# Doubles to single precision in two VectorE passes instead of three, inside an mLSTM and mixture-of-experts kernel

## The chip, the cores and the metric

One core of one Trainium2 chip. The metric is the device time of one execution in microseconds (us); lower is better. The core's engines are TensorE (PE in the profile; PEld is its weight load), VectorE (DVE), ScalarE (ACT), GpSimd (POOL) and SyncE (SP, which here only issues DMAs).

## The reference, cut to what matters

Three stages follow one another: an mLSTM attention with 4 x 8 heads over 768 positions and 40 columns a head, a dense two-layer network with 2048 hidden columns, and a mixture of 8 experts with one expert for each token.

```python
# attention, for every position t, in float32
m_new = np.maximum(f_gate[:, :, t] + m, i_gate[:, :, t])
C = f_stab[..., None, None] * C + i_stab[..., None, None] * np.einsum('bhd,bhe->bhde', vt, kt)
y[:, :, t] = o * np.einsum('bhde,bhe->bhd', C, qt) / denom
# dense layer: x is 3072 x 320
h = x @ w_in                                # w_in  320 x 2048
x = (h * (1.0 / (1.0 + np.exp(-h)))) @ w_out   # w_out 2048 x 320
# experts: one of 8 for each token, F = 1024
out[mask] = gate_w[mask, None] * (np.maximum(x[mask] @ w1[e], 0.0) @ w2[e])
```

The scale factor in `w_in` and `w_out` is a double, so both arrays come as doubles (64 bits an element), and the kernel first has to bring them to single precision. All other inputs are single precision.

## The kernel before, in words

The attention is computed in 6 chunks of 128 positions for 4 batches, which makes 24 tiles of 128 tokens (`unit(t)`). Each tile goes through the first dense layer (`l1`, `l1_two`), the second (`l2`, `l2_two`), the routing to an expert (`route`), and, sorted by expert in DRAM, through the experts (`slot`, `slot_two`). Values are split into a high and a low half-precision part (f16), and products are made of three terms of these parts.

Conversion of the doubles (`narrow`, L894) comes in 20 pieces of 128 x 512 elements. Ten are of `w_in` (`conv_in`, `conv_rest`), with two PSUM banks `cv_b` in turn and five staging tiles `t_b`. Ten are of `w_out` (`conv_out`), with the one PSUM bank `cvo_b` and three staging tiles `to_b`. A piece is loaded as pairs of 32-bit words into a staging tile T. Then VectorE makes a single-precision number in the PSUM bank by three passes on integers: L904 shifts the high word left by 3 and masks it, L907 adds the sign and the first exponent bit of the high word, and L910 adds the last three mantissa bits, which are the top bits of the low word. Behind that, the high f16 part is copied out (by ScalarE at L948, or by `scaled`, L75 on ScalarE and L77 on VectorE), TensorE subtracts it in the bank (`rest`, L923, and L970), and the remainder is copied out as the low part (`scaled` again). The first layer's products need the pieces of `w_in`; the second layer's need those of `w_out`.

The first 4 tiles (`unit(0)` to `unit(3)`) run beside the conversions. Their gates come from two scans for each part of the sequence (`gates`, L545 and L555, on VectorE), transposes (L594) and splits on GpSimd.

The order of the work is not the order of the program text. Each operation is entered with `op(engines, ns, ...)`: the engines that may do it, an estimated duration on each, what it reads and writes, a rank, and whether it uses the port that VectorE and GpSimd share in this model (`port`). `Plan.order` runs a list scheduler over the whole program eight times (`forward`, then new ranks from `backward`), keeps the shortest plan, and each engine executes its operations in that order. Where two engines are named, the plan also chooses the engine. The ranks of the first round come from the table `RK` (L28) and the position of the tile. Loads are issued on SP's queue in plan order, and each waits there until its buffer is free.

Of the kernel before, what the change touches and what calls it, by code (L numbers as in the profile page):

```python
# [10 lines left out]
F16 = mybir.dt.float16  # L11
BF16 = mybir.dt.bfloat16
I32 = mybir.dt.int32
AF = mybir.ActivationFunctionType
ALU = mybir.AluOpType
AX = mybir.AxisListType
# [9 lines left out]
SWG = 32.0  # L26
EX = 4
RK = dict(  # L28
    tiles=19.85, win=357.54, dwin=156.47, wout=226.1, dwout=-31.98, u0=-746.18, u1=-176.02, u2=-2598.68, u3=-1489.29,
    lead1=91.49, lead=1619.18, l1c=-760.87, l2c=-473.82, l2=-73.95, gates=-1631.02, load=-74.57, state=-183.26, route=-452.72,  # L30
)


# [5 lines left out]
def act(n):  # L39
    return 186 + 0.833 * n  # L40
# [6 lines left out]
def dve(n):  # L47
    return (n + 151) / 0.96


def pool1(n):
    return 85 + 1.3 * n
# [6 lines left out]
DP = ("DVE", "POOL")  # L59


def dp(n):
    return dve(n), pool2(n)
# [9 lines left out]
def scaled(nc, m, out, in_, scale):  # L73
    if m is nc.scalar:
        m.activation(out=out, in_=in_, func=AF.Copy, scale=scale)  # L75
    else:
# [211 lines left out]
def mlstm_moe_kernel(ctx, tc, q, k, v, ig, fg, og, w_in, w_out, w_gate, w1, w2, out):  # L288
    nc = tc.nc
# [18 lines left out]
    def op(*args, **kw):  # L308
        plan[0].op(*args, **kw)
# [27 lines left out]
    def pos(t):  # L337
        return T0 + TT * t
# [63 lines left out]
    for e in range(E):  # L402
        a = A[home[e]]
# [20 lines left out]
    fs, is_, ms, la, cl, rmask = [G0.cut([128, S], F32) for _ in range(6)]  # L424
    t_b = [A[0].cut([128, 1024], I32) for _ in range(5)]
    to_b = [A[1].cut([128, 1024], I32) for _ in range(3)]
    dg = A[1].cut([BH, NC, BH], F32)
# [10 lines left out]
    pe, ve, ac, po, sp = nc.tensor, nc.vector, nc.scalar, nc.gpsimd, nc.sync  # L438
# [68 lines left out]
    for e in sorted({e for e, _ in EARLY}):  # L507
        m = sum(1 for x in EARLY if x[0] == e)
# [12 lines left out]
       W=[("f", 0)], rank=-30, lag=2200, move=250)  # L521
    op("SP", 700, lambda: sp.dma_start(out=is_.ap[:, 0:CH], in_=bcast0(i2v[:, 0:CH], 128 // BH)),
       W=[("i", 0)], rank=-29, lag=2200, move=250)
    op("SP", 700, lambda: sp.dma_start(out=fs.ap[0:BH, CH:], in_=f2v[:, CH:]),
       W=[("f", 1)], rank=0, lag=2200, move=300)
    op("SP", 700, lambda: sp.dma_start(out=is_.ap[0:BH, CH:], in_=i2v[:, CH:]),
       W=[("i", 1)], rank=0, lag=2200, move=300)
# [115 lines left out]
    def unit(t):  # L643
# [3 lines left out]
        p = RK[f"u{t}"] if t < B else pos(t) - RK["lead1" if t < 2 * B else "lead"]  # L647
# [16 lines left out]
        if c > 0:  # L664
            op("SP", 450, lambda: [
                sp.dma_start(
                    out=lam[g].ap, in_=bcast0(lam_d[b * H + 4 * g:b * H + 4 * g + 4, c * CH:(c + 1) * CH], 128)
                ) for g in range(2)
            ], R=["lam_d"], W=[*lam], rank=ld + 3, lag=2500, move=1650)
            for g in range(2):  # L670
                op("POOL", pool1(512), lambda g=g: po.affine_select(  # L671
                    out=lam[g].ap, in_=lam[g].ap, pattern=[[0, 4], [1, CH]], compare_op=ALU.is_ge, fill=-1e30,
# [43 lines left out]
        for g in range(2):  # L716
            if c == 0:
                ps, kk = bank("at", 128, 4, CH)

                def first(g=g, ps=ps):  # L720
# [8 lines left out]
                   R=[kk], W=[lam[g]], rank=p + 2 + g)  # L729
            else:  # L730
                for j in range(4):
                    op("ACT", actp(128), lambda g=g, j=j: exps(4 * g + j, lam[g].ap[:, j, :]),
                       R=[("bias", 1)], W=[lam[g]], rank=p + 2 + g)

        if c > 0:
            op("ACT", act(H * D1), lambda: ac.activation(
                out=V2.ap[:, 0], in_=vr.ap, func=AF.Copy, scale=SQ
            ), R=[vr], W=[V2], rank=p + 4)
            op("DVE", dve(H * D1), lambda: ve.scalar_tensor_tensor(
                out=V2.ap[:, 1], in0=vr.ap, scalar=SQ, in1=V2.ap[:, 0], op0=ALU.mult, op1=ALU.subtract  # L740
            ), R=[vr], W=[V2], rank=p + 4, port=True)
        if c < NC - 1:
            op(DP, dp(H * D1), lambda m: m.tensor_tensor(
                out=vw.ap, in0=vr.ap, in1=wend_t[:, c, cols].unsqueeze(2).to_broadcast([128, H, D1]), op=ALU.mult
            ), R=[vr, ("wend", g_)], W=[vw], rank=p + 4, port=True)
        if 0 < c < NC - 1:
            op("ACT", act(H * D1), lambda: ac.copy(out=vv.ap[:, 0], in_=vw.ap), R=[vw], W=[vv], rank=p + 6)
            op(DP, dp(H * D1), lambda m: m.tensor_tensor(
                out=vv.ap[:, 1], in0=vw.ap, in1=vv.ap[:, 0], op=ALU.subtract
            ), R=[vw], W=[vv], rank=p + 6, port=True)  # L750
        op("ACT", act(320), lambda: ac.activation(out=orr.ap, in_=orr.ap, func=AF.Tanh, scale=0.5),
           W=[orr], rank=p + 8)
# [10 lines left out]
        for g in range(2):  # L763
            ps, kk = two[g]
            if c > 0:
# [6 lines left out]
                out=lam[g].ap, in0=ps, scalar=1.0 / SQ if c > 0 else SQ * SQ, in1=lam[g].ap,  # L772
                op0=ALU.mult, op1=ALU.mult
            ), R=[kk], W=[lam[g]], rank=p + 6 + g)
            if c == 0:
# [3 lines left out]
               R=[lam[g]], W=[P2], rank=p + 7 + g)  # L779
            op(DP, dp(512), lambda m, P2=P2, g=g: m.tensor_tensor(  # L780
                out=P2.ap[:, 1], in0=lam[g].ap, in1=P2.ap[:, 0], op=ALU.subtract
            ), R=[lam[g]], W=[P2], rank=p + 7 + g, port=True)
        if c > 0:
            it, ki = bank("at", 128, H, D1)

            def inter():
# [4 lines left out]
                out=hb.ap, in0=it, in1=E_t[:, c, cols].unsqueeze(2).to_broadcast([128, H, D1]), op=ALU.mult  # L791
# [15 lines left out]
        if c > 0:  # L807
            op("DVE", dve(H * D1), lambda: ve.tensor_tensor(out=pv, in0=pv, in1=hb.ap, op=ALU.add),
               R=[hb], W=[kv], rank=p + 10)

        def denom():
            nq = pv[:, :, D:D1]
            ve.tensor_scalar(
                out=dn.bitcast(I32), in0=nq.bitcast(I32), scalar1=0x7FFFFFFF, scalar2=None, op0=ALU.bitwise_and
            )
# [3 lines left out]
        y, ky = pv[:, :, 0:D], kv  # L819
        if c == 0:  # L820
            y, ky = hb.ap[:, :, 0:D], hb
            op(DP, (dve(160), pool1(320)), lambda m: m.tensor_scalar(
                out=orr.ap, in0=orr.ap, scalar1=1.0, scalar2=None, op0=ALU.add
            ), W=[orr], rank=p + 9, port=True)
            op(DP, dp(320), lambda m: m.tensor_tensor(
                out=orr.ap, in0=orr.ap, in1=den.to_broadcast([128, H, D]), op=ALU.mult
            ), R=[kd], W=[orr], rank=p + 11, port=True)
            op("DVE", dve(320), lambda: ve.tensor_tensor(out=y, in0=pv[:, :, 0:D], in1=orr.ap, op=ALU.mult),
               R=[kv, orr], W=[hb], rank=p + 11)
        else:  # L830
            op("DVE", dve(320), lambda: ve.scalar_tensor_tensor(
                out=y, in0=orr.ap, scalar=1.0, in1=y, op0=ALU.add, op1=ALU.mult
            ), R=[orr], W=[kv], rank=p + 11)
            op("DVE", dve(320), lambda: ve.tensor_tensor(
                out=y, in0=y, in1=den.to_broadcast([128, H, D]), op=ALU.mult
            ), R=[kd], W=[kv], rank=p + 11)
# [4 lines left out]
           W=[yy], rank=p + 12)  # L841
        op(DP if c == 0 else "DVE", dp(320) if c == 0 else dve(320), lambda m=ve: m.tensor_tensor(
            out=yl, in0=y, in1=yh, op=ALU.subtract
        ), R=[ky], W=[yy], rank=p + 12, port=c == 0)
        turned(yy, yy.ap.rearrange("p x c -> p (x c)"), xt, 6, p + 12, t < B - 1)
        if c < NC - 1:
# [15 lines left out]
            if c > 0:  # L862
                o = c * BH + b * H
                op(DP, dp(H * D1), lambda m: m.tensor_tensor(
                    out=C.ap, in0=C.ap, in1=dec[0:D, o:o + H].unsqueeze(2).to_broadcast([D, H, D1]), op=ALU.mult
                ), R=["dec"], W=[C], rank=rs - 4, port=True)
            op("PE", 24 * 30 if c else 920, state, R=[K, vv] if c else [kr, vw], W=[kk], rank=rs)
            if c > 0:
                op("DVE", dve(H * D1), lambda ps=ps: ve.scalar_tensor_tensor(
                    out=C.ap, in0=ps, scalar=1.0 / SQ, in1=C.ap, op0=ALU.mult, op1=ALU.add  # L870
                ), R=[kk], W=[C], rank=rs)
            else:
                op(AD, ad(H * D1), lambda m, ps=ps: scaled(nc, m, C.ap, ps, 1.0), R=[kk], W=[C], rank=rs)
            op("ACT", act(H * D1), lambda: ac.copy(out=Cs.ap[0:D], in_=C.ap),
               R=[C], W=[Cs], rank=rs + 4)
            op(DP, dp(H * D1), lambda m: m.tensor_tensor(
                out=cw.ap, in0=C.ap, in1=Cs.ap[0:D], op=ALU.subtract
# [9 lines left out]
    wpf = 2 if wide else 1  # L887
    win_v = w_in.bitcast(I32)
    wout_v = w_out.bitcast(I32)

# [3 lines left out]
    def narrow(T, X, mid, z, n, rank):  # L894

        if not wide:
            op("DVE", dve(n), lambda: ve.tensor_copy(out=z.ap.bitcast(I32), in_=T.ap[:, 0:n]), R=[T], W=[X, mid],
               rank=rank)
            return
        t4 = T.ap.rearrange("p (n w) -> p n w", w=2)  # L900
        lo, hi = t4[:, :, 0], t4[:, :, 1]
        a, m, o = X.ap.bitcast(I32), mid.ap.bitcast(I32), z.ap.bitcast(I32)
        sb = X.region != "PS"
        op("DVE", 150 + 0.78 * n if sb else dve(n), lambda: ve.tensor_scalar(  # L904
            out=a, in0=hi, scalar1=3, scalar2=0x3FFFFFFF, op0=ALU.logical_shift_left, op1=ALU.bitwise_and
        ), R=[T], W=[X], rank=rank, port=sb)
        op("DVE", dve(n), lambda: ve.scalar_tensor_tensor(  # L907
            out=m, in0=hi, scalar=-0x40000000, in1=a, op0=ALU.bitwise_and, op1=ALU.bitwise_or
        ), R=[T, X], W=[mid], rank=rank, port=sb)
        op("DVE", dve(n), lambda: ve.scalar_tensor_tensor(  # L910
            out=o, in0=lo, scalar=29, in1=m, op0=ALU.logical_shift_right, op1=ALU.bitwise_or
        ), R=[T], W=[X, mid], rank=rank, port=sb and mid is X)

    def opened():

# [526 lines left out]
    for t in range(2, B):  # L1442
# [4 lines left out]
       rank=12)  # L1447
# [33 lines left out]
    for t in range(1, NTT):  # L1481
# [24 lines left out]
        if t % B == 1 and t > 1:  # L1506
            next(ways, None)
            if t == NTT - B + 1:
# [3 lines left out]
                   R=["cum", "tri"], W=[kc], rank=pos(t) + 20)  # L1512
# [10 lines left out]
                for i, (e, n) in enumerate(EARLY):  # L1523
                    o = e * ER + 128 * (n + 1)
# [48 lines left out]
    def tabs():  # L1573
# [10 lines left out]
       rank=rk2)  # L1584

    def static_table():
# [9 lines left out]
       rank=rk2 + 1)  # L1596
# [126 lines left out]
```

## Time and profile before

| | |
|---|---|
| Median of 3 runs | 639.63 us (638.44 to 641.13) |
| Profiled execution | 638.35 us |
| Its span, from the first to the last instruction | 636.6 us |
| Mean granted TensorE clock | 0.988 |
| TensorE busy | 600.3 us, 94% of the span |
| VectorE busy | 488.2 us, 77% |
| ScalarE busy | 390.7 us, 61% |
| GpSimd busy | 309.8 us, 49% |

A row of a timeline gives start, duration, engine, line, operation, output and input, and in brackets the idle time of the engine ahead of it with what ended it. A row of waits gives who waited for whom, the total, how many times, and the longest. A row of a window table gives the stretch, its length, the busy time of each engine with the number of instructions, the granted TensorE clock as a share of full speed, the share of the 16 DMA engines, and GB/s.

### The profile page before, as it was taken

The page shows a single profiled execution, that of the slowest core. Times are in us where ns is not written, and L with a number is a line of the kernel's source. Part 1 is how long each engine was busy: PE and PEld are TensorE (multiplying, and loading weights), DVE is VectorE, ACT ScalarE, POOL GpSimd, SP SyncE. Part 2 cuts the span into 40 slices and gives each one's busy share as a digit, 9 for nine tenths or more (in the row PEclk, how much of TensorE's full clock was granted, in tenths as well). Part 3 has the DMA queues.
Part 4 walks back from the last instruction along what each step waited for, and adds up shares of the span by engine and source line. Part 5 has one row for each costly group of instructions (what it writes and reads, how often), then busy time and mean ns, then how long its engine had stood idle before and what let it go on. Part 6 is the DMA issues. An engine that isn't in the chain of part 4 may idle for free. (4 is left out here: it accounts for less than half of the span.)

```text
span 636.6 us, 17457 instructions
## 1 busy us (share of the span) xinstructions
PE 600.3 (94%) x6669; PEld 497.6 (78%) x6669; DVE 488.2 (77%) x986; ACT 390.7 (61%) x806; POOL 309.8 (49%) x462
## 2 busy tenths in 40 slices
PE   3889999999999989999999999999999899999992
PEld 2678888888888878878788887878788788888881
DVE  5997887889888788888798899757576675766660
ACT  2768897787778748888596755545432453644340
POOL 5537676557667568664764744511422214122311
PEclk9889999999999999999999999999999999999997
DMA  8999688999999969778876535582647889888610
GB/s 182 281 225 234 121 148 152 196 170 156 253 213 223 141 144 172 154 161 151 172 132 127 156 99 147 155 162 74 208 125 154 199 211 203 231 218 211 183 49 16
DMA packets 270006, 106.83 MB, mean 168 GB/s; under 512 B 207030, under 2 KB 265593, under 8 KB 269913
## 3 DMA queue, kind: packets, MB, share of 16 engines
q1 hardware_dynamic: 257176, 86.85, 67.1%
q10 hardware_dynamic: 9856, 10.10, 6.1%
q0 software_dynamic: 2880, 8.68, 3.8%
q8 instruction: 54, 0.88, 0.6%
q14 instruction: 40, 0.32, 0.2%
HBM read 68.76 MB, written 12.38 MB: 127 GB/s over the span
## 5 line engine op out<-in xcount | busy, mean ns | idle before, releaser
L1093 PE MATMUL PS<-A,A 128*128 128x256 f16 x1280 | 156.0, 272 | 0.6 <-DVE A L1097 0.6
L1093 PEld LDWEIGHTS <-A 128*128 128x128 f16 x1280 | 122.4, 98 | 17.6 <-issue 0.8
L1118 PE MATMUL PS<-A,A 128*128 128x320 f16 x320 | 95.7, 299 | 0.0
L1120 PE MATMUL PS<-A,A 128*128 128x320 f16 x320 | 95.6, 299 | 0.0
L1119 PE MATMUL PS<-A,A 128*128 128x320 f16 x320 | 95.6, 299 | 0.0
L1392 POOL DMA_INDIRECT out_dram<-W,sid x28 | 29.8, 1065 | 97.0 <-DVE W L1380 79.4
L1095 ACT ACTIVATE A<-PS 128x512 f32<-128x512 f32 x80 | 47.4, 594 | 36.5 <-PE PS L1093 31.2
L1097 DVE SCALAR_TENSOR_TENSOR A<-A,PS 128x512 f32<-128x512 f32 x80 | 54.1, 679 | 11.7 <-ACT A L1095 10.6
L1100 ACT CAST A<-A 128x512 f16<-128x512 f32 x80 | 49.1, 614 | 17.1 <-DVE A L1097 16.3
L712 ACT ACTIVATE A<-A,bias_t 128x128 f32<-128x128 f32 x160 | 56.0, 394 | 2.5 <-POOL A L671 2.4
L1416 PEld LDWEIGHTS <-A 128*128 128x128 f16 x512 | 49.7, 98 | 6.8
L1416 PE MATMUL PS<-W,A 128*128 128x256 f16 x448 | 52.7, 273 | 0.0
L1101 POOL TENSOR_TENSOR A<-A 128x512 f16<-128x512 f32 x28 | 35.1, 1254 | 31.6 <-ACT A L1100 31.6
L1354 PE MATMUL PS<-W,A 128*128 128x128 f16 x768 | 47.0, 219 | 2.6 <-DVE W L1358 1.8
L1354 PEld LDWEIGHTS <-A 128*128 128x128 f16 x768 | 44.8, 98 | 4.8 <-issue 3.1
L1418 ACT ACTIVATE W<-PS 128x512 f16<-128x512 f32 x32 | 19.1, 597 | 43.6 <-PE PS L1416 33.7
L1101 POOL TENSOR_TENSOR A<-A,A 128x512 f16<-128x512 f32 x24 | 28.5, 1188 | 29.7 <-ACT A L1100 28.2
L1356 ACT ACTIVATE W<-PS 128x512 f16<-128x512 f32 x24 | 14.2, 596 | 46.4 <-PE PS L1354 20.0
L771 DVE SCALAR_TENSOR_TENSOR A<-PS,A 128x512 f32<-128x512 f32 x48 | 32.2, 683 | 12.4 <-PE PS L769 11.3
L780 POOL TENSOR_TENSOR A<-A 128x512 f16<-128x512 f32 x25 | 31.5, 1259 | 19.2 <-ACT A L778 19.1
L1120 PEld LDWEIGHTS <-A 128*128 128x128 f16 x320 | 31.2, 98 | 12.2
L1430 PE MATMUL PS<-A,W 128*128 128x320 f16 x128 | 38.3, 299 | 0.5 <-DVE W L1380 0.5
(305 smaller groups left out, 1619.7 us busy)
## 6 DMA issues: line engine op xcount, KB each, us to landing
A<-lam_d SPq DMA_DIRECT2D x40, 256.0 KB
SG<-in_moe_w_dram SPq DMA_DIRECT2D x24, 320.0 KB
SG<-in_moe_w_dram SPq DMA_DIRECT2D x24, 256.0 KB
A<-in_moe_w_out_dram SPq DMA_DIRECT2D x10, 512.0 KB
A<-in_moe_w_in_dram SPq DMA_DIRECT2D x8, 512.0 KB
A<-in_k_dram SPq DMA_DIRECT2D x24, 160.0 KB
A<-in_q_dram SPq DMA_DIRECT2D x24, 160.0 KB
A<-in_v_dram SPq DMA_DIRECT2D x24, 160.0 KB
```

The lines of the kernel that those rows point to most:

```text
L712: ac.activation(out=lam[h // 4].ap[:, h % 4, :], in_=x, func=AF.Exp, bias=bias_t[:, c, b * H + h:b * H + h + 1])
L1093: pe.matmul(o, w[:, j, :], both[:, :, x, :], start=(n == 0), stop=(n == 7))
L1095: op("ACT", act(512), lambda: ac.activation(out=th.ap, in_=ps, func=AF.Tanh, scale=0.5 * HS), R=[kk], W=[th], rank=rk)
L1097: op("DVE", dve(512), lambda: ve.scalar_tensor_tensor(out=th.ap, in0=th.ap, scalar=1.0, in1=ps, op0=ALU.add, op1=ALU.mult), R=[kk], W=[th] ...
L1100: op("ACT", act(512), lambda: ac.copy(out=G.ap[:, 0], in_=th.ap), R=[th], W=[G], rank=rk + 2)
L1101: op(DP, dp(512), lambda m: m.tensor_tensor(out=G.ap[:, 1], in0=th.ap, in1=G.ap[:, 0], op=ALU.subtract), R=[th], W=[G], rank=rk + 2, port= ...
L1118: pe.matmul(ps, gh, w[:, 0, :], start=(f == 0), stop=False)
L1119: pe.matmul(ps, gh, w[:, 1, :], start=False, stop=False)
L1120: pe.matmul(ps, gl, w[:, 0, :], start=False, stop=(f == NF - 1))
L1354: pe.matmul(ps[:, jj, :], l, m, start=(n == 0), stop=(n == len(terms) - 1))
L1416: pe.matmul(o, a[:, k, :], both[:, :, x, :], start=(n == 0), stop=(n == 7))
L1430: pe.matmul(ps, hh[:, 0, 2 * f + b, :], x[:, 0, :], start=(g == 0 and f == 0), stop=False)
```

## The change

The second of the three passes is gone as a VectorE pass of its own. A new pass `three`, offered to GpSimd and ScalarE, reads the third 16-bit word of each double from above (the top half of the low word), scales it by 2^-13 with an offset that makes the rounding go down, and so writes its top three bits as an integer 0 to 7 into the low half of the high word, in place, in the staging tile. It comes behind the first VectorE pass, which still needs the old high word, and ahead of the last, which now takes the sign, the first exponent bit and these three bits from the high word with one mask. The masks of the first and last passes change to fit. The estimate for adding 1 to the output gate on GpSimd (L822) changes from 501 to 1012 ns, and all but one of the values in `RK` change, so the order of the whole program is computed anew.

```diff
@@ RK
-    tiles=19.85, win=357.54, dwin=156.47, wout=226.1, dwout=-31.98, u0=-746.18, u1=-176.02, u2=-2598.68, u3=-1489.29,
-    lead1=91.49, lead=1619.18, l1c=-760.87, l2c=-473.82, l2=-73.95, gates=-1631.02, load=-74.57, state=-183.26, route=-452.72,
+    tiles=19.85, win=453.55, dwin=151.6, wout=3.69, dwout=-20.45, u0=-751.86, u1=-141.04, u2=-3186.12, u3=-2421.48,
+    lead1=73.29, lead=1716.64, l1c=-997.71, l2c=-535.61, l2=-19.6, gates=-1783.78, load=-35.8, state=-251.22, route=-445.61,
@@ unit, chunk 0
-            op(DP, (dve(160), pool1(320)), lambda m: m.tensor_scalar(
+            op(DP, (dve(160), 1012), lambda m: m.tensor_scalar(
@@ narrow
-        lo, hi = t4[:, :, 0], t4[:, :, 1]
-        a, m, o = X.ap.bitcast(I32), mid.ap.bitcast(I32), z.ap.bitcast(I32)
+        hi = t4[:, :, 1]
+        a, o = X.ap.bitcast(I32), z.ap.bitcast(I32)
         sb = X.region != "PS"
         op("DVE", 150 + 0.78 * n if sb else dve(n), lambda: ve.tensor_scalar(
-            out=a, in0=hi, scalar1=3, scalar2=0x3FFFFFFF, op0=ALU.logical_shift_left, op1=ALU.bitwise_and
+            out=a, in0=hi, scalar1=3, scalar2=0x3FFFFFF8, op0=ALU.logical_shift_left, op1=ALU.bitwise_and
         ), R=[T], W=[X], rank=rank, port=sb)
+        t16 = T.ap.bitcast(U16).rearrange("p (n w) -> p n w", w=4)
+        low3, top = t16[:, :, 1], t16[:, :, 2]
+
+        def three(m):
+            if m is nc.scalar:
+                m.activation(out=top, in_=low3, func=AF.Copy, scale=2.0 ** -13, bias=-4095.5 * 2.0 ** -13)
+            else:
+                m.tensor_scalar(
+                    out=top, in0=low3, scalar1=4095.5, scalar2=2.0 ** -13, op0=ALU.subtract, op1=ALU.mult
+                )
+        op(("POOL", "ACT"), (85 + 3 * n, act(n)), three, W=[T], rank=rank, port=True)
         op("DVE", dve(n), lambda: ve.scalar_tensor_tensor(
-            out=m, in0=hi, scalar=-0x40000000, in1=a, op0=ALU.bitwise_and, op1=ALU.bitwise_or
-        ), R=[T, X], W=[mid], rank=rank, port=sb)
-        op("DVE", dve(n), lambda: ve.scalar_tensor_tensor(
-            out=o, in0=lo, scalar=29, in1=m, op0=ALU.logical_shift_right, op1=ALU.bitwise_or
-        ), R=[T], W=[X, mid], rank=rank, port=sb and mid is X)
+            out=o, in0=hi, scalar=-0x3FFFFFF9, in1=a, op0=ALU.bitwise_and, op1=ALU.bitwise_or
+        ), R=[T, X], W=[X, mid], rank=rank, port=sb)
```

## Rows read from the trace of the kernel before

**Rows 1.** Page, busy time of each engine, share of the span, instructions.
```profile
PE 600.3 (94%) x6669; PEld 497.6 (78%) x6669; DVE 488.2 (77%) x986; ACT 390.7 (61%) x806; POOL 309.8 (49%) x462
```

**Rows 2.** Windows by stage: length, PE, PEld, DVE, ACT, POOL, PEclk, DMA, GB/s.
```profile
0.00:20.00 20.00, 9.26 (x54) 5.88 (x54) 12.38 (x27) 7.24 (x15) 12.70 (x43) 1.00 0.91 197
20.00:60.00 40.00, 35.54 (x420) 30.27 (x421) 35.09 (x66) 28.73 (x61) 19.34 (x32) 0.91 1.02 245
60.00:100.00 40.00, 38.74 (x566) 33.51 (x564) 34.71 (x69) 34.96 (x83) 27.68 (x43) 1.00 0.73 147
100.00:620.00 520.00, 511.73 (x5601) 424.54 (x5600) 404.27 (x824) 319.74 (x651) 248.16 (x345) 1.00 0.78 167
620.00:636.60 16.60, 5.00 (x37) 3.38 (x35) 1.76 (x3) 0.00 (x0) 1.96 (x2) 0.74 0.05 16
```

**Rows 3.** First and last pass of `narrow`: ns minimum/median/maximum, first and last start.
```profile
L904 DVE TENSOR_SCALAR PS<-A x20: 673/686/695, 6.0 to 75.4; 128x512 int32<-128x512 int32 x20
...
L910 DVE SCALAR_TENSOR_TENSOR PS<-A,PS x20: 673/689/695, 9.7 to 79.5; 128x512 int32<-128x512 int32 x20
```

**Rows 4.** TensorE's waits: who for whom, total us, times, longest.
```profile
PE PS L594 <- DVE W L555: 3.0, 1, 3.0
...
PE PS L694 <- DVE PS L904: 1.5, 1, 1.5
PE PS L923 <- DVE A L77: 1.3, 1, 1.3
PE PS L1062 <- ACT A L75: 0.6, 1, 0.6
...
PE PS L1217 <- DVE cum L1212: 1.5, 1, 1.5
```

**Rows 5.** Windows of 4 us around TensorE's two gaps.
```profile
24.00:28.00 4.00, 1.98 (x19) 1.44 (x17) 4.00 (x8) 2.91 (x6) 2.31 (x5) 0.92 1.14 308
28.00:32.00 4.00, 4.00 (x35) 2.99 (x35) 3.93 (x8) 3.66 (x8) 0.74 (x1) 0.66 1.02 216
40.00:44.00 4.00, 2.25 (x18) 1.30 (x16) 3.96 (x9) 3.19 (x8) 1.16 (x3) 1.00 0.75 134
44.00:48.00 4.00, 4.00 (x33) 3.44 (x33) 4.00 (x8) 1.86 (x5) 1.98 (x3) 0.57 1.22 306
```

**Rows 6.** Timeline of VectorE, passes of conversions.
```profile
7.29 0.67 DVE L907 SCALAR_TENSOR_TENSOR PS<-A,PS 128x512 int32<-128x512 int32 x1
...
9.71 0.68 DVE L910 SCALAR_TENSOR_TENSOR PS<-A,PS 128x512 int32<-128x512 int32 x1
...
27.43 1.29 DVE L910 SCALAR_TENSOR_TENSOR PS<-A,PS 128x512 int32<-128x512 int32 x2
```

**Rows 7.** Windows of L904 alone (VectorE busy, count), and its fifth start.
```profile
0.00:20.00 20.00, 2.77 (x4) 1.00 0.91 197
20.00:60.00 40.00, 8.12 (x12) 0.91 1.02 245
...
20.38 0.68 DVE L904 TENSOR_SCALAR PS<-A 128x512 int32<-128x512 int32 x1
```

**Rows 8.** Groups by line: busy us, mean ns, idle before and releaser.
```profile
L1040 ACT CAST A<-A 128x512 f16<-128x512 f32 x6 | 3.7, 621 | 0.4 <-DVE A L1037 0.4
...
L822 POOL TENSOR_SCALAR A<-A 128x320 f32<-128x320 f32 x4 | 4.1, 1017 | 4.5 <-ACT A L751 4.5
...
L973 POOL COPY A<-SG 64x512 f16<-64x512 f16 x3 | 1.8, 609 | 0.1
```

**Rows 9.** Timelines of VectorE and GpSimd, one line with and without neighbour.
```profile
74.52 0.90 DVE L739 SCALAR_TENSOR_TENSOR A<-A 128x328 f16<-128x328 f32 x1
89.92 0.49 DVE L739 SCALAR_TENSOR_TENSOR A<-A 128x328 f16<-128x328 f32 x1
...
74.27 0.81 POOL L748 TENSOR_TENSOR A<-A,A 128x328 f16<-128x328 f32 x1 [0.24 <-ACT A L747]
...
90.20 1.24 POOL L780 TENSOR_TENSOR A<-A 128x512 f16<-128x512 f32 x1 [2.66 <-ACT A L778]
```

More of the change, by code (lines that the diff above doesn't have):

```diff
@@ L13 @@
 I32 = mybir.dt.int32
+U16 = mybir.dt.uint16
 AF = mybir.ActivationFunctionType
```

## The prediction

> **What bounds the kernel now.** I read the engine totals first, then the stages, then who TensorE waits for. TensorE is busy for 600.3 of the 636.6 us, far more than any other engine [rows 1]. The stage table tells where the other 36.3 us lie [rows 2]: 10.7 us in the first 20, 4.5 between 20 and 60, 1.3 between 60 and 100, 8.3 in the long stretch from 100 to 620, and 11.6 behind the last product. From 100 to 620 TensorE is busy for 511.7 of 520 us, so there the time is TensorE's work and little else; no VectorE pass that goes can shorten that work. What a faster VectorE can win lies before 100 us, and that is where all 20 conversions of the doubles are: their passes start between 6.0 and 79.5 us [rows 3], and VectorE is busy there for 35.1 of the 40 us from 20 to 60 [rows 2].
>
> TensorE's waits before 100 us give the places [rows 4]. It waits 3.0 us for the gate scan (L555), 1.5 us until a conversion's first pass lets a PSUM bank go (L904), 1.3 us for a half-precision copy of a converted weight (L77 on VectorE), and 0.6 us at the second layer's first products of a tile for a copy of the output weights (L75 on ScalarE). The second loss is the clock. In the stretch from 24 to 28 us TensorE is busy for only 2.0 of 4.0 us, and from 28 to 32 the granted clock is 0.66; from 40 to 44 it is busy for 2.3, and from 44 to 48 the clock is 0.57 [rows 5]. [...]
>
> **The change part by part.** *VectorE passes.* Each conversion had three passes of 128x512, 20 of each kind, 0.69 us at the median of the first and the last kind [rows 3]; two in a row take 1.29 us, so one more costs 0.60 [rows 6]. Twenty go: 12.0 us of VectorE time, of which 12 x 0.60 = 7.2 us between 20 and 60, where 12 conversions are opened [rows 7]. The mask of the first pass and the operands of the second change nothing in their form: 0 us.
>
> *The added pass.* Twenty passes of 512 16-bit elements, 8 bytes apart, in SBUF, on GpSimd or ScalarE, whichever the written order finds free. No row has this form. On ScalarE the nearest row is an SBUF-to-SBUF cast of 128x512 at 0.62 us [rows 8]; I take 0.6, bounded by 0.6 and, if the step halves the rate, 1.2. On GpSimd the nearest is the one-input arithmetic pass of L822, 1.02 us for 320 elements; by length 512/320 x 1.02 = 1.63 us. The bounds are the 512-element copy at 0.61 us and, since two operations are asked where L822 has one, twice 1.63 = 3.3 us. I take 1.6. ScalarE is busy for 28.7 and GpSimd for 19.3 of the 40 us from 20 to 60 [rows 2], so half of the passes on each (some 6 x 0.6 = 3.6 and 6 x 1.6 = 9.6 us there) finds room. That cover is gone where a pass stands in front of a copy for which TensorE waits.
>
> [...]
>
> *The chain of one conversion.* Two passes on one engine become VectorE, other engine, VectorE. Three passes took 0.60 + 0.60 + 0.69 = 1.9 us; now it is 0.69 + 0.6 + 0.69 = 2.0 us by ScalarE and 0.69 + 1.6 + 0.69 = 3.0 by GpSimd, before any queueing. So a conversion is longer by 0.1 to 1.1 us (2.8 at the upper bound), while its PSUM bank and its staging tile are held, and the loads behind it in SP's in-order queue wait as much longer.
>
> *The order.* The starting ranks in RK, the cost given for the +1 on the output gate, and the new operation enter the order that is computed for the whole program. The +1 passes are four of 1.02 us on GpSimd [rows 8]; on VectorE they would be under 0.7 us each (the price of a 512-element pass). For the moved ranks I set 0 us. The bounds are the idle time that an order can make or mend after 100 us: at best its 8.3 us would go [rows 2], and at worst as much comes in again; by the single wait, 1.5 us at L1217 [rows 4] is what one misplaced step costs, and I take both signs as equally likely.
>
> *The sum, against the profiled execution.* Gate scan: of the three passes of the first conversion, two stand between the scans (L907 at 7.29, L910 at 9.71 us [rows 6]); one goes, -0.6 us. The two waits on VectorE between 20 and 60: the passes removed before 24 us (five conversions opened [rows 7], 5 x 0.60 = 3.0 us) exceed the first wait of 1.5, and the next 4 us removed exceed the second of 1.3, so both go, -2.8. Of the 3.4 us lost at the lower clock I take half, -1.7, because other short waits remain there. From 60 to 100: the last 20 - 4 - 12 = 4 passes of 0.60 go [rows 7], but only 1.3 us of idle time is there to win; -0.5. What is late next: one conversion by GpSimd on TensorE's path, +1.2 (the 1.1 of the chain and 0.1 of hand-over). Together -4.4 us. The profiled execution took 638.35 us in all, 1.75 beyond its span, so it would take 633.95; the median of the runs is 639.63, 1.28 above the profiled one, so I forecast 639.63 - 4.4 = 635.2 us.
>
> **The rivals.** *Nothing passes through.* VectorE's passes were hidden, or the loads take their place: the DMA engines' share is 1.02 from 20 to 60 us [rows 2]. For it: the serial path of the first batches goes through all engines. Against it: the two waits name VectorE. Then only the 0.6 of the gate scan is left, about 639.0 us.
>
> *Everything goes.* Both gaps, all of the low clock behind them, and both passes ahead of the gate scan: 2.8 + 3.4 + 1.2 + 1.3 us = 8.7, so 630.9 us.
>
> *The port.* A VectorE pass with two SBUF inputs is stretched when GpSimd works: L739 takes 0.90 us beside GpSimd's L748 and 0.49 with GpSimd idle [rows 9], a difference of 0.41. If each of ten GpSimd passes met one such VectorE pass, 4.1 of the 12.0 us saved would be paid back and the gain shrinks to 4.4 x 7.9 / 12.0 = 2.9: 636.7 us. Against it: the conversion's own passes read or write PSUM and take 0.69 us everywhere, and two-input SBUF passes crowd only after 60 us. [...]
>
> *Slower: the output weights come late.* All ten output conversions share one PSUM bank, so their chains are serial, and TensorE already waits 0.6 us for one of them (L1062 [rows 4]), so there is no slack at that point. If the last three, after 60 us, go by GpSimd at 1.6 us behind its masks and subtractions, each is 1.1 us later, 3.3 us in all; TensorE has run out of first-layer products, idles that long and loses another 1.7 at the lower clock as behind the earlier gaps. With nothing won earlier but the gate scan that is +4.4: 644.0 us. It decides from the point where the added delay exceeds what the saved VectorE time brought forward; at GpSimd's upper bound of 3.3 us it would be twice the idle time.
>
> **How the numbers follow.** My forecast has 0.45, with a range of its own from 632.0 to 637.5; nothing passes through 0.20; everything goes 0.10; the port 0.10; the output weights 0.15. The 0.5% that a measurement of this kernel can tell is 3.2 us, so faster means under 636.4 and slower over 642.8. Faster: 0.40 of the forecast's 0.45, all of "everything", 0.05 of the port: 0.55. Slower: the output weights and a little for a bad order, 0.17. The rest, 0.28, is the same. The range runs from 630.5, just below "everything goes", to 642.5, which leaves out most of the slower rival.
>
> **What would show it.** Right: two passes of 0.69 us per conversion on VectorE, VectorE's busy time down by 13 us; TensorE's idle time before 100 us down from 16.5 to about 12; the stretches at a low granted clock between 24 and 48 us shorter; the time after 100 us unchanged to 2 us. Wrong: GpSimd's added pass over 2 us or TensorE's waits naming it; a wait at L1062 of several us; VectorE less busy before 60 us but TensorE idle as long as before; or idle time after 100 us that moved by more than all of these.

## The result and the profile after

The changed kernel takes 650.25 us at the median (648.75 to 650.56) against 639.04 for the kernel before beside it: a ratio of 1.0142 (95% interval 1.0108 to 1.0175), where 635.2 was forecast with a range up to 642.5. The profiled execution's span is 648.9 us, 12.3 more than before, and its mean granted clock 0.974.

The engines' totals of the kernel after, to be laid beside [rows 1]:

```profile
PE 605.7 (93%) x6668; PEld 500.4 (77%) x6669; DVE 491.1 (76%) x984; ACT 402.9 (62%) x811; POOL 324.9 (50%) x459
```

VectorE should have lost 13 us and has 2.9 more. Twenty passes are gone, but before 100 us its busy time falls by 5.3 us only, because the new order gave it other work (six passes of L1050 there instead of two, 4.5 us more): GpSimd is 15.1 us busier although its added passes alone take 22.6. Behind 100 us VectorE is 8.2 us busier, partly with the same passes: the 24 of L1221 take 10.2 us instead of 5.1. The stages answer to [rows 2], with the same columns:

```profile
0.00:20.00 20.00, 9.70 (x54) 6.00 (x54) 11.70 (x29) 10.00 (x16) 9.87 (x36) 1.00 0.87 205
20.00:60.00 40.00, 30.86 (x314) 25.36 (x316) 29.79 (x52) 29.10 (x51) 27.47 (x24) 0.74 1.05 239
60.00:100.00 40.00, 37.82 (x542) 33.18 (x542) 35.40 (x63) 35.19 (x73) 30.34 (x48) 1.00 0.75 132
100.00:620.00 520.00, 510.78 (x5598) 422.88 (x5596) 404.55 (x827) 323.54 (x666) 252.42 (x346) 1.00 0.80 167
```

TensorE's idle time grew from 36.3 to 43.2 us, by 6.9: before 100 us from 16.5 to 21.6, 4.7 of these 5.2 between 20 and 60, and by 1.7 behind 100 us. The other 5.4 of the 12.3 us are TensorE's busy time, 605.7 us instead of 600.3 for the same products. The granted clock between 20 and 60 fell from 0.91 to 0.74. By these shares alone that is 40 x 0.17 = 6.8 us, but they count the lower clock also where TensorE stood idle. That the clock makes up all of the 5.4 is not shown: a version below (no pass added, first set) is busy for 604.8 us with a clock of 0.91 in that stretch. VectorE, which was to be relieved, is the less busy one in that stretch, 29.8 us against 35.1: the time was not lost to a full VectorE, but to waits and the clock.

The two engines' versions of the added pass (all their instructions: minimum, median and maximum in ns, first and last start), the last pass as a group, and the waits behind it:

```profile
L913 ACT ACTIVATE A<-A x12: 1336/1358/1402, 5.6 to 89.3; 128x512 uint16<-128x512 uint16 x12
L915 POOL TENSOR_SCALAR A<-A x8: 2659/2695/3738, 17.5 to 80.9; 128x512 uint16<-128x512 uint16 x8
```

```profile
DVE PS L919 <- POOL A L915: 5.0, 5, 2.2
...
DVE PS L919 <- ACT A L913: 2.6, 2, 1.4
...
PE PS L932 <- ACT A L76: 8.3, 2, 6.3
PE PS L640 <- POOL A L841: 3.3, 1, 3.3
```

The added pass takes 1.36 us on ScalarE and 2.70 on GpSimd. The order reckons with 0.61 and 1.62. VectorE, which executes in its written order, waits 7.6 us for it (L919 is the last pass), and TensorE waits for copies that stand behind it on the two engines. Both places can be followed. First ScalarE, then TensorE, in timelines:

```profile
24.37 1.34 ACT L913 ACTIVATE A<-A 128x512 uint16<-128x512 uint16 x1
25.73 1.21 ACT L76 ACTIVATE A<-PS 64x512 f16<-64x512 f32 x2
```

```profile
26.99 1.07 PE L932 MATMUL PS<-A,less 128*128 128x512 f16 x2 [2.03 <-ACT A L76]
...
48.95 0.29 PE L640 MATMUL PS<-ident,A 128*128 128x128 f16 x1 [3.29 <-POOL A L841]
```

TensorE waits 2.03 us for a copy by L76 that comes right behind an added pass (the other 6.3 us of L932's wait lie at the first conversion, where the kernel without the added pass, below, has 6.1). The second wait, of 3.29 us, is for GpSimd's L841, a copy of 0.24 us. GpSimd's and VectorE's timelines ahead of it:

```profile
41.34 3.74 POOL L915 TENSOR_SCALAR A<-A 128x512 uint16<-128x512 uint16 x1
45.14 0.18 POOL L583 COPY A<-W 32x5 f32<-32x5 f32 x1
45.41 0.45 POOL L584 TENSOR_TENSOR A<-A,ident 32x160 f32<-32x160 f32 x1
45.94 2.66 POOL L915 TENSOR_SCALAR A<-A 128x512 uint16<-128x512 uint16 x1
48.65 0.24 POOL L841 COPY A<-A 128x64 f16<-128x64 f16 x1
```

```profile
40.96 1.64 DVE L556 TENSOR_TENSOR_SCAN W<-W 32x640 f32<-32x640 f32 x1
...
48.63 0.70 DVE L919 SCALAR_TENSOR_TENSOR PS<-A,PS 128x512 int32<-128x512 int32 x1 [2.23 <-POOL A L915]
```

Two added passes run with hardly a gap from 41.34 to 48.60, 7.3 us, which the order reckons as 2 x 1.62 and small work; L841 and VectorE's last pass, which waited for the second of them, both begin at 48.6. Behind these two gaps the clock is low, as behind those of [rows 5]; windows of the same form:

```profile
20.00:24.00 4.00, 3.83 (x22) 3.24 (x23) 3.22 (x9) 2.26 (x4) 1.62 (x3) 0.62 1.15 301
24.00:28.00 4.00, 1.97 (x18) 1.25 (x16) 2.62 (x5) 3.93 (x7) 1.21 (x2) 0.50 1.19 251
28.00:32.00 4.00, 3.03 (x21) 2.20 (x20) 3.05 (x5) 3.18 (x6) 3.21 (x3) 0.60 1.16 304
...
44.00:48.00 4.00, 1.54 (x15) 0.98 (x14) 1.46 (x3) 1.87 (x4) 3.77 (x4) 0.61 1.13 242
48.00:52.00 4.00, 2.32 (x13) 1.53 (x15) 3.26 (x7) 2.56 (x6) 3.80 (x7) 0.50 1.20 230
52.00:56.00 4.00, 4.00 (x37) 3.46 (x36) 1.92 (x4) 3.28 (x5) 2.42 (x3) 0.61 1.08 245
```

From 44 to 52 us TensorE is busy for 3.9 of 8 us, and until 56 the clock stays between 0.50 and 0.61. The first low stretch begins already in the window from 20, ahead of the gap at 24.

### The profile page after: what moved, and what is told of

Same layout as the page of the kernel before. It is cut to its first block, busy times and chain, and to the rows that moved or that the text cites. A ratio compares the mean times of both kernels' runs of the same rounds, so it can differ in the third digit from the quotient of the medians.

```text
span 648.9 us, 17478 instructions
## 1 busy us (share of the span) xinstructions
PE 605.7 (93%) x6668; PEld 500.4 (77%) x6669; DVE 491.1 (76%) x984; ACT 402.9 (62%) x811; POOL 324.9 (50%) x459
## 4 chain that ended last, share of the span: by engine, by line
PE 71%; DVE 12%; POOL 5%; issue 5%; DMA 3%; ACT 1%; SPq 1%; another core or an unknown queue 0%; ACTq 0%; POOLq 0%; DVEq 0%
PE PS L1102 17%; PE PS L1425 8%; PE PS L1127 5%; PE PS L1129 5%; PE PS L1128 5%; PE PS L1363 5%; PE PS L1439 2%; PE PS L1440 2%; PE PS L1441 2%; PE PS L1042 2%; POOL A L915 2%; PE PS L1376 2%; PE PS L1378 2%; PE PS L1377 2%; DVE A L1106 1%
## 5 line engine op out<-in xcount | busy, mean ns | idle before, releaser
L1109 ACT CAST A<-A 128x512 f16<-128x512 f32 x80 | 48.7, 614 | 16.5 <-DVE A L1106 15.8
L781 POOL TENSOR_TENSOR A<-A 128x512 f16<-128x512 f32 x34 | 41.6, 1226 | 19.7 <-ACT A L779 19.7
L1110 POOL TENSOR_TENSOR A<-A 128x512 f16<-128x512 f32 x26 | 31.6, 1216 | 26.5 <-ACT A L1109 23.5
```

Source lines behind the costliest of these rows:

```text
L1109: op("ACT", act(512), lambda: ac.copy(out=G.ap[:, 0], in_=th.ap), R=[th], W=[G], rank=rk + 2)
L1110: op(DP, dp(512), lambda m: m.tensor_tensor(out=G.ap[:, 1], in0=th.ap, in1=G.ap[:, 0], op=ALU.subtract), R=[th], W=[G], rank=rk + 2, port= ...
```

## The experiments

Theory: the added pass is longer than the order reckons with, stands in front of other work on two in-order queues, and TensorE idles and then runs at the lower clock, as in the windows above. Rivals: the new ranks made a bad order, or the split of a conversion over two engines costs by its hand-overs. Ratios are to the kernel before, run on the same chip in the same rounds.

**Order alone.** The three passes of before, with the new ranks and the new price of L822:

```diff
-    tiles=19.85, win=357.54, dwin=156.47, wout=226.1, ...
+    tiles=19.85, win=453.55, dwin=151.6, wout=3.69, ...
```

> The three VectorE passes of before, with the changed start ranks and the changed price of the +1 pass. Theory A (the added pass is longer than the order reckons with: 2.7 us on GpSimd and 1.36 us on ScalarE in the changed kernel's trace, against 1.62 and 0.61 in the order): there is no added pass here, so about the time of before, 637 to 642 us. Theory B (the new start ranks give a poor order whatever the passes cost): 647 to 652 us. Theory C (a conversion that hands over to another engine and back holds VectorE's in-order queue, however long the added pass is): 637 to 642 us.

636.36 us against 636.94, ratio 0.9994 (0.9975 to 1.0012). For three passes the new ranks are as good as the old ones; the ranks lose nothing by themselves, only together with the added pass.

**The pass cut to its price.** The changed kernel, its order untouched; the pass works on fewer elements:

```diff
-                m.activation(out=top, in_=low3, ...
+                m.activation(out=top[:, 0:186], in_=low3[:, 0:186], ...
-                    out=top, in0=low3, ...
+                    out=top[:, 0:302], in0=low3[:, 0:302], ...
```

> The changed kernel in its own order, but the added pass covers only the first 186 elements on ScalarE and the first 302 on GpSimd, so that it should last the 0.61 and 1.62 us that the order reckons with (by 2.3 and 5.1 ns per element); the last three mantissa bits of the other elements are left wrong. Theory A: the loss is gone, 633 to 640 us. Theory B: 647 to 652 us, the order is the same. Theory C: most of the loss stays, 645 to 650 us.

637.67 us against 636.94, ratio 1.0007 (0.9987 to 1.0028). The pass in this kernel:

```profile
L913 ACT ACTIVATE A<-A x12: 616/624/652, 5.6 to 85.2; 128x186 uint16<-128x186 uint16 x12
...
L915 POOL TENSOR_SCALAR A<-A x8: 1677/1694/2748, 16.7 to 76.1; 128x302 uint16<-128x302 uint16 x8
```

All hand-overs are still there, and the whole loss is gone: it came from the length of the pass. VectorE's waits for the pass fall from 7.6 to 2.4 us. But the forecast gain does not come either.

**One engine at a time.** The first cut alone on GpSimd (302 elements), then alone on ScalarE (186).

> The changed kernel in its own order, with only GpSimd's eight added passes cut to 302 elements (1.7 us instead of 2.7); ScalarE's twelve keep 512 (1.36 us). The last three mantissa bits of the elements left out stay wrong. Theory A1 (GpSimd's passes carry the loss: in the changed kernel's trace VectorE waits 5.0 us for them, and TensorE 3.3 us for a copy that stands behind one in GpSimd's queue): 637 to 642 us. Theory A2 (ScalarE's passes carry it): 646 to 650 us. If both add up: 642 to 646 us.

> The same with only ScalarE's twelve passes cut to 186 elements (0.62 us instead of 1.36); GpSimd's eight keep 512. Theory A1: 646 to 650 us. Theory A2: 637 to 642 us. If both add up: 642 to 646 us.

645.20 and 644.10 us against 640.21; ratios 1.0077 (1.0048 to 1.0106) and 1.0054 (1.0025 to 1.0084). From 1.0142 the cut on GpSimd takes 0.65%, that on ScalarE 0.88%; together 1.53%, which ends at 0.9989, where both cuts at once gave 1.0007. Within these intervals of 0.3% the two excesses add up, and neither engine's (12 x 0.74 us on ScalarE, 8 x 1.0 on GpSimd) is shown to weigh more.

**No added pass at all,** the order untouched (the operation is planned and issues nothing):

```diff
         def three(m):
+            return
```

> The changed kernel in its own order with no added pass at all: the last three mantissa bits of the converted weights are left wrong, and each conversion is two VectorE passes with nothing between. Theory A (only the length beyond what the order reckons with costs): 634 to 638 us, about the 637.7 us of the run with the pass as long as reckoned. Theory C (the hand-over to another engine and back costs by itself): clearly under that run, 628 to 634 us.

638.95 us against 640.21, ratio 0.9982 (0.9959 to 1.0005). So the forecast's best case in this order, two passes of VectorE and nothing added, is worth 0.2%, at most 0.4% and perhaps nothing. It is 0.25% under the run with the pass cut to its price, inside the intervals, so the hand-overs by themselves cost little, and the 628 to 634 us of theory C did not come. Its stretch from 20 to 60 us, and windows of 4 us, below them two windows of the kernel before:

```profile
20.00:60.00 40.00, 36.59 (x407) 31.15 (x408) 32.84 (x63) 27.57 (x55) 13.68 (x19) 0.83 1.00 232
...
16.00:20.00 4.00, 3.34 (x31) 2.32 (x28) 2.78 (x6) 2.15 (x4) 0.74 (x1) 1.00 1.07 356
20.00:24.00 4.00, 4.00 (x30) 3.52 (x31) 3.30 (x9) 1.46 (x3) 1.32 (x2) 0.56 1.15 296
24.00:28.00 4.00, 3.34 (x20) 2.24 (x19) 3.79 (x8) 3.17 (x7) 1.17 (x3) 0.50 1.09 244
```

```profile
16.00:20.00 4.00, 3.42 (x37) 2.54 (x35) 3.88 (x8) 3.19 (x6) 3.78 (x4) 1.00 1.12 254
20.00:24.00 4.00, 3.63 (x39) 3.02 (x40) 3.93 (x8) 2.62 (x7) 2.24 (x5) 1.00 1.08 340
```

Idle time between 20 and 60 us fell from 4.5 to 3.4 us, but the clock there is 0.83 instead of 0.91: by these shares 40 x 0.08 = 3.2 us more lost. Over the whole span TensorE idles 32.8 us instead of 36.3 and is busy for 603.0 instead of 600.3: of 3.5 us won in waits 2.7 are paid back as longer busy time. The clock falls in the window from 20 although TensorE was busy for 3.34 of the 4 us before it (3.42 in the kernel before, where it did not fall).

**The pass by itself.** A kernel of nothing but such passes, four of each form; it computes nothing of the reference:

```
ac.activation(out=u4(a0, 2), in_=u4(a0, 1), func=AF.Copy, ...)   # L44: as in the kernel
ac.activation(out=u1(a1),    in_=u4(a0, 1), ...)                 # L48: written densely
ac.activation(out=u4(a1, 2), in_=u1(a0), ...)                    # L50: read densely
ac.activation(out=i2(a1, 0), in_=u4(a0, 1), ...)                 # L54: 32-bit words written at the same step
```

> No part of the computation: nine forms of the pass on ScalarE and nine on GpSimd, four times each, 512 elements, nothing beside them. Theory P1 (the write of 2 bytes at a step of 8 is what costs): on ScalarE 1.36 us wherever the output is 16-bit at a step, 0.6 us for a dense or a 32-bit output; on GpSimd likewise less with a dense output. Theory P2 (the read at a step costs): 0.6 us with a dense input whatever the output. Theory P3 (16-bit integers cost, at any step): 1.36 us for all 16-bit forms, 0.6 for 32-bit floats. On GpSimd also: if the second operation costs, the one-operation form at the same steps is under 2 us.

Groups by line (busy us, mean ns, idle time before). L44 to L54 as above; GpSimd: L65 as in the kernel, L69 written densely, L71 read densely, L73 both dense, L75 one operation instead of two:

```profile
L65 POOL TENSOR_SCALAR P<-P 128x512 uint16<-128x512 uint16 x4 | 10.7, 2666 | 4.0 <-DVE P L22 3.7
...
L71 POOL TENSOR_SCALAR P<-P 128x512 uint16<-128x512 uint16 x4 | 10.5, 2628 | 0.3
L75 POOL TENSOR_SCALAR P<-P 128x512 uint16<-128x512 uint16 x4 | 8.9, 2215 | 0.3
L69 POOL TENSOR_SCALAR P<-P 128x512 uint16<-128x512 uint16 x4 | 7.8, 1946 | 0.3
...
L73 POOL TENSOR_SCALAR P<-P 128x512 uint16<-128x512 uint16 x4 | 7.7, 1923 | 0.3
...
L44 ACT ACTIVATE A<-A 128x512 uint16<-128x512 uint16 x4 | 5.5, 1377 | 0.0
L50 ACT ACTIVATE A<-A 128x512 uint16<-128x512 uint16 x4 | 5.3, 1335 | 0.1
...
L54 ACT ACTIVATE A<-A 128x512 int32<-128x512 uint16 x4 | 2.6, 661 | 0.1
...
L48 ACT ACTIVATE A<-A 128x512 uint16<-128x512 uint16 x4 | 2.6, 656 | 0.1
```

The write is what costs: 16-bit elements written 8 bytes apart take 0.7 us more than written side by side, on both engines (1377 against 656, 2666 against 1946 ns), and 32-bit words at the same step do not on ScalarE (661). The read at that step is nearly free (1946 against 1923). On GpSimd the second operation adds another 0.45 (2666 against 2215), though the one-operation form is not under 2 us as expected.

**Another write, in the kernel.** 32-bit words over the low word, all else as after:

```diff
-        low3, top = t16[:, :, 1], t16[:, :, 2]
+        low3, top = t16[:, :, 1], t4[:, :, 0]
```

> The changed kernel with its own order and prices; the added pass reads the same 16-bit words, but writes 32-bit integers, one over each whole low word, instead of 16-bit ones into half of the high word, so the last three mantissa bits stay those of the high word. The passes measured alone (m1_forms) give it 0.66 us on ScalarE and about 1.95 us on GpSimd, instead of 1.36 and 2.7. Theory (the time is lost to the 16-bit write at a step of 8 bytes): ScalarE's pass takes 0.65 to 0.70 us, GpSimd's 1.9 to 2.2, VectorE's waits for them fall from 7.6 us to under 2, and the time is 638 to 642 us beside 639 for the kernel before. Rival (it is the engine change as such, or the read of the half words, that costs): 646 to 651 us, with passes as long as before.

641.56 us against 641.04, ratio 1.0028 (0.9999 to 1.0057). All its added passes:

```profile
L913 ACT ACTIVATE A<-A x12: 657/676/702, 4.8 to 82.7; 128x512 int32<-128x512 uint16 x12
...
L915 POOL TENSOR_SCALAR A<-A x8: 1979/1999/3064, 15.7 to 72.8; 128x512 int32<-128x512 uint16 x8
```

Same engines, same order, same 512 elements and same reads: inside the kernel too the passes are as short as the form of the write makes them, and most of the loss is gone. But the edit takes away more than the form. The last pass does not read the low words, so it no longer waits for the added pass (VectorE's waits for it are gone, from 7.6 us), and the added pass no longer waits for the first: on ScalarE it begins at 4.78 us, ahead of VectorE's first pass at 4.86, where in the kernel after it begins at 5.63, behind it. GpSimd's and VectorE's timelines for the conversion whose last pass waited 2.23 us in the kernel after:

```profile
41.13 1.98 POOL L915 TENSOR_SCALAR A<-A 128x512 int32<-128x512 uint16 x1
41.16 0.68 DVE L919 SCALAR_TENSOR_TENSOR PS<-A,PS 128x512 int32<-128x512 int32 x1
```

So this run confirms the price of the write, but its time does not part the shorter pass from the hand-over that is gone. What ties the loss to the length is the run with the pass cut to its price, which keeps the hand-overs.

**True prices, and old ranks.** The order is told 2700 and 1360 ns with the ranks of after; and the ranks of before with the prices of after:

```diff
-        op(("POOL", "ACT"), (85 + 3 * n, act(n)), three, ...
+        op(("POOL", "ACT"), (2700, 1360), three, ...
```

> The changed kernel with the order computed from the measured prices of the added pass (2700 ns on GpSimd, 1360 ns on ScalarE). Theory A: the order now places the pass where there is room, so most of the loss is gone, 636 to 644 us; what remains is the real work, 20 times 0.75 to 1.1 us more than reckoned. Theory B and theory C: 646 to 652 us.

> The changed kernel with the start ranks of before; the added pass keeps its low prices in the order. Theory A: still late, 645 to 652 us. Theory B: the loss is gone, 636 to 641 us. Theory C: 645 to 652 us.

659.59 us, ratio 1.0361 (1.0313 to 1.0409), and 661.93, ratio 1.0418 (1.0366 to 1.0469). Both lie above every range that was expected. A true price alone made it worse, and so did the old ranks: the ranks were good for the program and the prices they stood with. In the first of these VectorE's waits for GpSimd's pass did fall to 1.9 us, but TensorE idles for 16.6 us from 100 to 620 instead of 9.2 in the kernel after, 7.7 of it far behind the conversions, at a single step of the experts (in the second, VectorE waits 9.4 us for GpSimd's pass instead of 5.0):

```profile
PE PS L1439 <- ACT W L1427: 7.7, 1, 7.7
```

**Ranks fitted anew.** To part the pass from the order, ranks were fitted by a search, twice each for the true prices, for two passes with nothing added (last three mantissa bits zero), and for the three passes of before (with the new price of L822).

> The changed conversion with the measured prices of the added pass (2700 and 1360 ns) in the order, and start ranks fitted anew to these prices by a search over some 2,600 sets. The earlier run with true prices kept ranks that were fitted to the low ones. Theory A (the added pass is late where the order reckons it short): placed with its true length it does much less harm, 638 to 646 us; faster than before only if GpSimd's and ScalarE's room before 100 us is really free. Theory D (true prices make the order worse by themselves, whatever the ranks): 652 to 662 us, as in that run.

> The changed kernel with the added pass as it is, entered into the order at 2700 ns on GpSimd and 1360 on ScalarE, and a second set of ranks fitted for these prices. Theory (the slow pass itself costs little once the order knows of it; what is left is the scatter of orders): 636 to 643 us, as the first set gave 640.3. Rival (the slow pass costs whatever the order): 645 us or more.

> Two VectorE passes for each conversion and no added pass in the order either; the last three mantissa bits of the converted weights are zero. Start ranks fitted in the same way. If the 12 us of VectorE time before 100 us are worth something once the order knows that they are free: 630 to 635 us. If TensorE's start is bound by loads and by the serial path of the first batches: 635 to 640 us, as before.

> As the run with two passes and no added pass, with another set of ranks that the same search found from another start: how much two orders of one program differ. Within 3 us of it if the fitted orders are alike; more if the order matters more than VectorE's 12 us.

> The three passes of before with start ranks fitted by the same search: what the search alone is worth. If the ranks of before are about as good as the search finds: 635 to 641 us. If the search alone wins: 630 to 635 us, and the run without the added pass has to be read against this one.

> The kernel before, its three passes kept, with a second set of ranks fitted for it anew. Theory (the 4 us of e11_no_pass_refit2 come from VectorE's freed passes): no fitted order of the three passes gets there, 635 to 640 us. Rival (the order alone scatters by that much): 631 to 634 us.

| version | first set | second set |
|---|---|---|
| pass at its true price | 640.31, 1.0067 (1.0045 to 1.0088) | 643.32, 1.0021 (0.9997 to 1.0046) |
| no pass added | 637.53, 1.0008 (0.9983 to 1.0033) | 631.98, 0.9937 (0.9915 to 0.9959) |
| three passes of before | 636.32, 1.0006 (0.9986 to 1.0027) | 640.15, 0.9975 (0.9949 to 1.0002) |

The kernel before is 636.48 us beside all but the two second sets of 640.15 and 643.32, where it is 641.04. With ranks made for it the kernel with the slow pass is 0.2% (not clear of nothing) to 0.7% over the kernel before, not 1.4. One version beats both kernels, the second without the pass, by 0.6%. Its windows:

```profile
20.00:60.00 40.00, 36.66 (x394) 30.36 (x395) 32.24 (x61) 26.70 (x55) 18.00 (x23) 0.80 0.90 221
...
100.00:620.00 520.00, 516.19 (x5646) 428.05 (x5644) 404.02 (x834) 321.77 (x655) 247.05 (x341) 1.00 0.78 168
```

Its idle time after 100 us is 3.8 us instead of 8.3, while the clock between 20 and 60 is lower than before (0.80 against 0.91). These 4.5 us are won far from the conversions. Before 100 us it idles 3.6 us less, but TensorE's busy time is 3.1 us longer (603.4). None of the three orders of three passes tried here (0.9994, 1.0006 and 0.9975) got as low, which speaks for VectorE's freed time; but the two sets of one version lie 0.7% apart, so the order alone can account for as much, and that the gain is VectorE's freed time is not shown.

## Why the prediction was wrong

*What bounds the kernel.* Right in the main: 5.2 of the 6.9 us of added idle time are before 100 us, and the lower clock is in the stretch from 20 to 60.

*VectorE's passes.* The 20 passes went as reckoned, but VectorE's busy time between 0 and 100 us fell from 82.2 to 76.9 us, not by 12 (the list of signs says 13): the order moved work onto it.

*The added pass: the step that failed.* 0.6 us was taken on ScalarE with an upper bound of 1.2; it is 1.36, outside. On GpSimd 1.6 was taken and 3.3 bounded; it is 2.70. The bound on ScalarE came from a cast that writes its elements side by side [rows 8], and the halved rate was thought of as a matter of the step in general. The runs put it on the write of 16-bit elements (1377 against 656 ns on ScalarE), and with the pass cut to the assumed length the loss of 1.4% is gone (ratio 1.0007). Half of the passes were reckoned on each engine; 12 went to ScalarE and 8 to GpSimd.

*The chain.* 0.69 + 1.36 + 0.69 = 2.7 us and 0.69 + 2.70 + 0.69 = 4.1 us instead of 2.0 and 3.0. The sentence that the cover is gone where a pass stands in front of a copy for which TensorE waits named the mechanism; it was priced once, at 1.2 us for one conversion, and came at two places with 2.0 and 3.3 us of waiting. By the test written down (GpSimd's pass over 2 us, TensorE's waits behind it), the prediction is wrong by the cause it named itself.

*The ranks.* 0 us was right for three passes (ratio 0.9994). With the added pass they are worth more than the bound of 8.3 us: the old ranks give a ratio of 1.0418 where the new ones give 1.0142. What was missed is that ranks and prices are one fit: a pass at another length than its price makes the whole order wrong for the chip, and correcting the price alone cost 3.6%.

*The sum.* Also wrong by itself: with the pass as short as assumed the gain of 4.4 us (0.7%) would have had to show, and 0.9987 to 1.0028 excludes it. Without the pass the first 20 us gave 0.9 us (0.6 forecast), the waits from 20 to 60 gave 1.1 of the 2.8, and the low clock cost 3.2 more by its share (TensorE's busy time is 2.7 longer), where 1.7 less was forecast. No run shows the 3.4 us lost at the lower clock, of which the sum takes half (the rivals take all, or the 1.7 of one gap): they were an estimate from the clock shares of [rows 5], 4 x (0.08 + 0.34 + 0.43), and in their place the run without the pass shows the 3.2 us more. Half of the lost clock was credited to the removal of two waits, but in the new order TensorE's clock falls at another place (0.56 from 20 to 24 us, where it was 1.00 in the kernel before). Apart from the length of the pass, "nothing passes through", at 639.0 us and 0.20, was the case that came.

*The other rivals.* "The output weights come late" had the kind of mechanism (a late chain, TensorE idle, then a clock of 0.50 to 0.61), at L932 and L640 instead of L1062, and 644.0 was too little. What the port rival expected of VectorE's passes showed on the other side: GpSimd's pass was stretched, by 1.05 us (3.74 against 2.69), where it began 0.38 us behind a scan of VectorE; that a shared port does it is not shown. That two-input passes in SBUF "crowd only after 60 us" left these scans out, of which the kernel before has one at 21.56 us.

*Open.* Why the clock falls in the window from 20 us in the kernel after and in those with its order, with TensorE about as busy ahead of it as before. A low stretch between 20 and 60 us is in every version (mean clock 0.74 to 0.91), with its place and length changing with the order; no run was made to hold it still. Nor does a run part what VectorE's waits for the pass cost from what the copies queued behind it cost; both go with its length.

## What to carry to other kernels

A pass moved off a busy engine pays only if its price there is known in its exact form: element size, step of the write and number of operations (here the form of the write alone made 1.38 us out of 0.66 on ScalarE); measure it alone before planning with it. Where each engine executes a fixed order, a pass longer than its price delays everything behind it on two queues, and that can cost several times what the busy engine saved (here 1.4%, against 0.2% for the saved passes in the same order). And before crediting a gain to removed work, take the work out without replacement in the same order: here that bounded the gain at 0.4% in the order as it was.

## What the runs showed of the hardware

ScalarE writes 512 elements of 16 bits 8 bytes apart in 1.34 to 1.39 us, twice the 0.66 of the same pass written densely or as 32-bit words; GpSimd pays the same 0.7 us (2.67 against 1.95 written densely).

GpSimd's pass was stretched by a scan on VectorE (its two operands both lie in SBUF) by the same amount in three kernels. VectorE's and GpSimd's rows of the kernel with the shortened pass, and of that with 32-bit words:

```profile
39.04 1.64 DVE L556 TENSOR_TENSOR_SCAN W<-W 32x640 f32<-32x640 f32 x1
...
39.43 2.75 POOL L915 TENSOR_SCALAR A<-A 128x302 uint16<-128x302 uint16 x1
```

```profile
36.82 1.64 DVE L556 TENSOR_TENSOR_SCAN W<-W 32x640 f32<-32x640 f32 x1
...
37.21 3.06 POOL L915 TENSOR_SCALAR A<-A 128x512 int32<-128x512 uint16 x1
```

It is 1.05 and 1.07 us over the medians of 1.69 and 2.00, as it was 1.05 over 2.69, whatever the pass's own length; the scan had 1.25 us left each time. In the kernel with the old ranks a pass began 0.18 us behind another scan, which had 1.35 us left, and took 3.83 us, 1.14 over its median; so the loss is each time 0.2 us less than what was left of the scan. It went with the rest of the scan and not with the length of the pass. The other way round, one scan was stretched and another was not. A scan that began while GpSimd's two-input pass L826 had 0.64 us left took 1.99 us (second set of ranks for the true prices) instead of the 1.47 beside an idle GpSimd (old ranks, and the scan at 21.56 us in the kernel before). Behind the added pass, which has one input, nothing of the kind shows; VectorE's and GpSimd's rows of the kernel after:

```profile
33.19 1.53 DVE L546 TENSOR_TENSOR_SCAN W<-W 32x640 f32<-32x640 f32 x1
...
32.31 2.69 POOL L915 TENSOR_SCALAR A<-A 128x512 uint16<-128x512 uint16 x1 [1.04 <-DVE PS L905]
```

Here GpSimd's pass was first and ran on until 35.00, and the scan that began 0.88 us behind it took 1.53 us, as it does in the kernel with 32-bit words where GpSimd is idle beside it; neither was stretched.
